# Attention, two expert layers: the order in which a pair's sums and reciprocals are emitted

## The chip, the core and the metric

The kernel runs on one core of one Trainium2 chip. The metric is the device time of one execution in microseconds (us), the median of the runs shown. A core has a matrix engine (PE, with its weight loads listed as PEld), a vector engine (DVE), an activation engine (ACT), a general engine (POOL) and a queue that issues transfers (SP). Each of them works through its own list of instructions in order and waits where an input or a buffer is not there yet.

## What is computed

Attention over 4 batches and 12 heads, with sequences of 448 and heads of 64, comes first. Its output, read as 1792 tokens of 768, goes through a dense two-layer network and then through one that sends each token to one of 8 experts. The change touches only the attention:

```python
def rmsnorm(x, g):
    rms = np.sqrt(np.mean(x * x, axis=-1, keepdims=True) + 1e-06)
    return x / rms * g
q_n, k_n = (rmsnorm(q, g_q), rmsnorm(k, g_k))
scores = scale * np.matmul(q_n, k_n.transpose(0, 1, 3, 2))
scores = scores - np.max(scores, axis=-1, keepdims=True)
attn = np.exp(scores)
attn = attn / (np.sum(attn, axis=-1, keepdims=True) + 1e-09)
return np.matmul(attn, v).astype(np.float32)
```

## The kernel before, in words

The attention works on 24 pairs of heads. The 448 keys of a pair lie in four chunks of 112. One pass of the loop in `pieces` (lines 363 to 383) walks through the names in `ORDER` (line 385), and each name emits a piece of work for one of several pairs: the current one, the one before it, the next one, or one further ahead.

- `Uk` and `Uq` (`turn_k`, `turn_q`, lines 228 to 244) turn the normalised keys and queries of the pair two passes ahead on PE into a PSUM buffer named `tr` (line 225). ACT copies the high part (`kh` L242, `qh` L233), and DVE takes the low part (`kl` L243, `ql` by the helper on L63).
- `P0` to `P3` (`probs`, line 262) make the scores of one chunk of the current pair: eight PE matmuls into the one `sc` buffer (L273; `SCB` is 1) and the exponential on ACT (L275). The first chunk's result goes into `pr`, the other three into `p`.
- `V0` to `V3` (`values`, line 278) multiply a chunk's probabilities with the values on PE (L284) into `av`. From the second chunk on POOL adds `p` to `pr` (L288). So a pair has three additions, the last one behind `P3`.
- `S` (`sums`, line 290) belongs to the pair before. PE sums `pr` over the keys (L296, 16 small matmuls into a `tr` buffer), ACT copies the result (L300), PE brings it back into columns (L303), and DVE takes the reciprocals `r` (L306).
- `C` (`close`, line 309) belongs to the pair before too. PE spreads `r` (L314, 16 small matmuls into a `tr` buffer), ACT copies it (`rt`, L318), DVE multiplies `av` with it (L320), ACT and DVE split the result into a high and a low part (`xTh` L322, `xTl` on L63).
- `T0` to `T3` (`top`, L250 and L252) find the maxima of the scores of the next pair: two PE matmuls into the one `tp` buffer and a DVE reduction. `R` (`row`, L257 and L259) turns the maxima by way of a `tr` buffer.
- `A` (line 366) prepares later pairs: loads of q, k and v on SP (L173, L174), squares on ACT (`sq`, L192) and their sums on DVE (`ms`, L193) for two pairs at a time, a chain of small DVE operations for the reciprocal root (L195 to L201) and the product on POOL (`qn`, L216). `sq` and `qn` share one tag with three buffers.

There are two `tr` buffers, used by `Uk`, `S`, `C`, `Uq` and `R` in turn, two `av` and two `pr` buffers. The text of the program gives the emission order; a scheduler places the instructions on the engines, and emission order ranks them. In the last six passes the attention overlaps with the decoding of weights for the dense network (`decode`, line 399), whose first transfers are emitted behind the last load of the attention (line 646).

Of the kernel before, what the change touches and what calls it, by code (L numbers as in the profile page):

```python
# [20 lines left out]
def attention_moe_moe2(  # L21
# [17 lines left out]
    B, H, S, DH = q.shape  # L39
# [111 lines left out]
    class Attention:  # L151
# [173 lines left out]
        def pieces(self):  # L325
# [37 lines left out]
            for i in range(n + 1):  # L363
                for op in ORDER:
                    cur, prev, nxt = (sts[m] if 0 <= m < len(sts) else None for m in (i, i - 1, i + 1))
# [16 lines left out]
                        self.row(nxt)  # L382
                    yield

    ORDER = "Uk P0 S P1 C V0 T0 P2 V1 T1 P3 Uq V2 A T2 T3 R V3".split()
    BANK, HALVES = 512, (slice(0, DH), slice(DH, P))
    SCB, AVB, TRB = 1, 2, 2
    QK, VV, PB, RT, WD, RAW, D0, DS, NU, L0, LA, U0, US, LW, XL, SD = 3, 2, 3, 1, 1, 3, 18, 2, 2, -2, 2, 5, 4, 3, 1, 0
# [254 lines left out]
    for i, _ in enumerate(att.pieces()):  # L643
        step = i // len(ORDER)
        if step >= D0 and i % (DS * len(ORDER)) == 0 and len(wts.raw) < RAW:
            wts.decode(att.last)
# [298 lines left out]
```

## Time and profile before

| what | value |
|---|---|
| median of 3 runs | 1267.56 us (1266.53 to 1269.69) |
| the profiled execution, its time | 1269.48 us |
| its span from first to last instruction | 1267.8 us |
| granted TensorE clock, mean | 0.974 of full speed |
| stretch in which the attention runs steadily | about 94 to 302 us of the span |
| dense network, steady | about 500 to 880 us |
| expert network | about 920 to 1268 us |

The profile lists for each engine when an instruction was busy, how long the engine stood idle before it, and which instruction's end released it. An idle gap costs time only where the work behind it lies on the path that sets the end. A wait for several things is put down to the one that came last.

### The profile page before, as it was taken

To read this page: it belongs to the slowest core of one execution; us is meant where nothing else is said; L and a number is where in the kernel's file an instruction comes from. 1 tells how busy PE (TensorE), PEld (TensorE's weight loads), DVE (VectorE), ACT (ScalarE), POOL (GpSimd) and SP (SyncE) were. 2 spreads that over 40 slices of the span, in tenths; PEclk is the share of its full clock that TensorE was granted. 3 is DMA by queue.
4 is the path that set the end of the run, shared out by engine and by line. 5 is a ranking of instruction groups with operands and counts; after the bars stand their busy time and mean duration, and the time that the engine had idled before them with its cause. 6 is when DMAs were issued, how large, how long until landed. Compare 5 with 4: busy or idle time off the path is not lost.

```text
span 1267.8 us, 19050 instructions
## 1 busy us (share of the span) xinstructions
PE 1173.1 (93%) x6988; PEld 935.8 (74%) x6988; DVE 783.3 (62%) x1291; ACT 500.9 (40%) x791; POOL 544.1 (43%) x366
## 2 busy tenths in 40 slices
PE   4899998989888998999999999999799999999997
PEld 2445554545466887898989898988678888898986
DVE  7576777766765788485858584335656159414456
ACT  3355655555433532222222222122335158314444
POOL 2656666766553554343434443120224136312334
PEclk9889999999888999999999999999889999999999
DMA  4112111210222222021202120062276039512556
GB/s 103 51 50 62 45 52 44 59 37 16 65 63 63 75 78 72 13 75 38 70 31 75 38 63 1 1 218 59 74 283 223 34 120 359 210 46 84 185 214 219
DMA packets 68081, 116.28 MB, mean 92 GB/s; under 512 B 6780, under 2 KB 45948, under 8 KB 67968
## 3 DMA queue, kind: packets, MB, share of 16 engines
q1 hardware_dynamic: 64848, 103.87, 25.6%
q0 software_dynamic: 3120, 11.02, 2.5%
q8 instruction: 57, 0.93, 0.3%
q14 instruction: 56, 0.46, 0.1%
HBM read 106.61 MB, written 12.58 MB: 94 GB/s over the span
## 4 chain that ended last, share of the span: by engine, by line
PE 61%; DVE 17%; POOL 8%; issue 5%; ACT 4%; DMA 3%; SPq 1%; ACTq 0%; DVEq 0%; POOLq 0%
PE mp L485 5%; PE mo L466 5%; PE mp L486 5%; PE mo L467 5%; PE mp L487 5%; PE mo L468 5%; PE ph L823 4%; PE ph L822 3%; PE ph L821 3%; PE sc L273 3%; PE av L284 3%; PE py L839 3%; PE py L837 3%; PE py L838 3%; POOL pr L288 2%
## 5 line engine op out<-in xcount | busy, mean ns | idle before, releaser
L288 POOL TENSOR_TENSOR pr<-pr,p 112x896 f32<-112x896 f32 x72 | 160.2, 2225 | 89.9 <-ACT p L275 81.5
L493 DVE TENSOR_TENSOR ysum<-mp,ysum 128x448 f32<-128x448 f32 x168 | 103.6, 620 | 114.9 <-PE mp L487 114.0
L485 PE MATMUL mp<-gh,w1h 128*128 128x448 f32 x384 | 144.9, 379 | 15.5 <-DVE ysum L493 12.8
L466 PE MATMUL mo<-xTh,w0h 128*128 128x448 f32 x384 | 143.3, 373 | 4.8 <-DVE g L473 4.6
L486 PE MATMUL mp<-gl,w1h 128*128 128x448 f32 x384 | 142.7, 372 | 0.0
L467 PE MATMUL mo<-xTl,w0h 128*128 128x448 f32 x384 | 142.3, 370 | 0.0
L468 PE MATMUL mo<-xTh,w0l 128*128 128x448 f32 x384 | 142.1, 370 | 0.0
L487 PE MATMUL mp<-gh,w1l 128*128 128x448 f32 x384 | 141.4, 371 | 0.1
L63 POOL TENSOR_TENSOR gl<-g,gh 128x448 fp32r<-128x448 f32 x64 | 78.0, 1218 | 134.8 <-ACT gh L474 107.5
L252 DVE TENSOR_REDUCE md<-tp 112x2 f32<-112x896 f32 x96 | 104.3, 1087 | 18.4 <-PE tp L250 18.4
L425 POOL TENSOR_TENSOR raw<-raw,top 128x384 f32<-128x384 f32 x64 | 64.8, 1012 | 114.1 <-DVE raw L423 111.6
L837 PE MATMUL py<-w2h,hT 128*128 128x384 f32 x288 | 99.7, 346 | 0.0
L839 PE MATMUL py<-w2l,hT 128*128 128x384 f32 x288 | 96.8, 336 | 0.0
L838 PE MATMUL py<-w2h,hL 128*128 128x384 f32 x288 | 96.5, 335 | 0.0
L485 PEld LDWEIGHTS mp<-gh,w1h 128*128 128x128 f32 x384 | 73.0, 190 | 29.0 <-DVE ysum L493 14.8
L63 DVE TENSOR_TENSOR hL<-pt,hT 128x512 fp32r<-128x512 f32 x36 | 24.8, 689 | 106.2 <-ACTq L847 59.3
L823 PE MATMUL ph<-w1l,xgh 128*128 128x512 f32 x216 | 86.3, 400 | 4.2 <-DVE w1l L63 4.2
L275 ACT ACTIVATE p<-sc 112x896 f32<-112x896 f32 x72 | 65.8, 914 | 53.7 <-PE sc L273 53.4
L821 PE MATMUL ph<-w1h,xgh 128*128 128x512 f32 x216 | 86.6, 401 | 0.3 <-ACT xgh L799 0.3
L419 ACT ACTIVATE mag<-wd 128x384 f32<-128x384 f32 x64 | 35.5, 555 | 128.6 <-DVE raw L426 109.7
L822 PE MATMUL ph<-w1h,xgl 128*128 128x512 f32 x216 | 85.5, 396 | 0.0
L466 PEld LDWEIGHTS mo<-xTh,w0h 128*128 128x128 f32 x384 | 72.9, 190 | 13.5 <-DVE g L473 6.3
(195 smaller groups left out, 2567.4 us busy)
## 6 DMA issues: line engine op xcount, KB each, us to landing
r<-in_moe_w_dram SPq DMA_DIRECT2D x27, 1024.0 KB, 5.3
r<-in_moe_w_dram SPq DMA_DIRECT2D x36, 768.0 KB, 7.4
wd<-in_moe_w_in_dram SPq DMA_DIRECT2D x32, 384.0 KB, 3.3
wd<-in_moe_w_out_dram SPq DMA_DIRECT2D x32, 384.0 KB, 3.0
qk<-in_q_dram SPq DMA_DIRECT2D x24, 224.0 KB, 2.9
qk<-in_k_dram SPq DMA_DIRECT2D x24, 224.0 KB, 3.2
vv<-in_v_dram SPq DMA_DIRECT2D x24, 224.0 KB, 3.0
x2d<-xn SPq DMA_DIRECT2D x24, 224.0 KB, 2.9
```

The costliest lines, as they stand in the source:

```text
L288: nc.gpsimd.tensor_tensor(st["pr"][:CP], st["pr"][:CP], p, ALU.add)
L466: nc.tensor.matmul(ph, wh_[:, c], xh, start=(c == 0), stop=False)
L467: nc.tensor.matmul(ph, wh_[:, c], xl, start=False, stop=False)
L468: nc.tensor.matmul(ph, wl_[:, c], xh, start=False, stop=(c == KD - 1))
L485: nc.tensor.matmul(py, hi[:, sl], gh, start=(j == 0), stop=False)
L486: nc.tensor.matmul(py, hi[:, sl], gl, start=False, stop=False)
L487: nc.tensor.matmul(py, lo[:, sl], gh, start=False, stop=(j == GF - 1))
L821: nc.tensor.matmul(ph[n], xh[:, c], w1h[:, c, s_], start=(c == 0), stop=False)
L823: nc.tensor.matmul(ph[n], xh[:, c], w1l[:, c, s_], start=False, stop=(c == K1 - 1))
L837: nc.tensor.matmul(py[n], hT[:, c], w2h[:, c, s_], start=(c == 0), stop=False)
L838: nc.tensor.matmul(py[n], hL[:, c], w2h[:, c, s_], start=False, stop=False)
L839: nc.tensor.matmul(py[n], hT[:, c], w2l[:, c, s_], start=False, stop=(c == K2 - 1))
```

## The change

One line differs. `S` moves from behind `P0` to behind `P2`. `C` moves from behind `P1` to behind `Uq`, which itself follows `P3`. No operation is added or removed.

```diff
-    ORDER = "Uk P0 S P1 C V0 T0 P2 V1 T1 P3 Uq V2 A T2 T3 R V3".split()
+    ORDER = "Uk P0 P1 V0 T0 P2 S V1 T1 P3 Uq C V2 A T2 T3 R V3".split()
```

## Rows read from the trace of the kernel before

**Rows 1.** The page: busy time of the engines over the span.
```profile
PE 1173.1 (93%) x6988; PEld 935.8 (74%) x6988; DVE 783.3 (62%) x1291; ACT 500.9 (40%) x791; POOL 544.1 (43%) x366
```

**Rows 2.** Busy time by stretch; the first line names the columns.
```profile
core 0: us, PE busy (x) PEld busy (x) DVE busy (x) ACT busy (x) POOL busy (x), PEclk, DMA share, GB/s
94.00:302.00 208.00, 189.16 (x1632) 106.28 (x1632) 151.07 (x250) 117.07 (x169) 135.14 (x77) 1.00 0.17 48
...
500.00:880.00 380.00, 372.75 (x1929) 333.90 (x1928) 223.47 (x418) 94.11 (x167) 130.51 (x103) 1.00 0.19 57
```

**Rows 3.** All waits of PE from 94 to 302 us: sum, times, longest.
```profile
PE tr L296 <- POOL pr L288: 14.6, 16, 1.5
PE tr L314 <- DVE r L306: 4.2, 7, 0.6
```

**Rows 4.** Timeline of PE, one pass from 200.44 us (start, duration, operation).
```profile
201.15 0.36 PE L273 MATMUL sc<-mx,mask 64*112 64x448 f32 x2
201.35 0.37 PE L250 MATMUL tp<-kh,qh 64*112 64x448 f32 x2
203.24 0.59 PE L296 MATMUL tr<-pr,ones_mat 113*32 113x112 f32 x16 [1.53 <-POOL pr L288]
203.76 0.46 PE L273 MATMUL sc<-qh,kh 64*112 64x448 f32 x2
...
205.67 0.55 PE L303 MATMUL av<-ident,sp 128*112 128x4 f32 x4
...
208.16 0.94 PE L314 MATMUL tr<-ident,r 112*64 112x112 f32 x16
209.03 0.60 PE L225 MATMUL tr<-ident,qn 112*128 112x112 f32 x4
...
211.66 0.60 PE L257 MATMUL tr<-ident,md 112*128 112x112 f32 x4
212.20 0.46 PE L250 MATMUL tp<-kh,qh 64*112 64x448 f32 x2
212.59 0.60 PE L225 MATMUL tr<-ident,qn 112*128 112x112 f32 x4
```

**Rows 5.** Timeline of PE, from a pass of the other kind.
```profile
161.71 0.59 PE L296 MATMUL tr<-pr,ones_mat 113*32 113x112 f32 x16 [0.46 <-POOL pr L288]
...
167.60 0.60 PE L314 MATMUL tr<-ident,r 112*64 112x112 f32 x8 [0.61 <-DVE r L306]
```

**Rows 6.** Timeline of POOL.
```profile
194.66 2.04 POOL L216 TENSOR_TENSOR qn<-qk,y 112x512 f32<-112x512 f32 x2 [1.03 <-DVE y L201]
196.67 2.10 POOL L288 TENSOR_TENSOR pr<-pr,p 112x896 f32<-112x896 f32 x1
198.72 2.44 POOL L216 TENSOR_TENSOR qn<-qk,y 112x512 f32<-112x512 f32 x2
201.12 2.07 POOL L288 TENSOR_TENSOR pr<-pr,p 112x896 f32<-112x896 f32 x1
...
212.58 2.92 POOL L288 TENSOR_TENSOR pr<-pr,p 112x896 f32<-112x896 f32 x1 [1.88 <-ACT p L275]
```

**Rows 7.** Timeline of ACT.
```profile
203.96 0.35 ACT L300 COPY sp<-tr 128x224 f32<-128x224 f32 x1 [1.49 <-PE tr L296]
204.93 0.92 ACT L275 ACTIVATE p<-sc 112x896 f32<-112x896 f32 x1 [0.63 <-PE sc L273]
...
209.67 0.55 ACT L233 ACTIVATE qh<-tr 128x448 fp32r<-128x448 f32 x1
210.11 1.05 ACT L192 ACTIVATE sq<-qk 112x1024 f32<-112x1024 f32 x1
```

**Rows 8.** Timeline of DVE.
```profile
206.26 0.21 DVE L306 RECIPROCAL r<-av 112x8 f32<-112x8 f32 x1 [3.41 <-PE av L303]
...
209.72 0.62 DVE L320 TENSOR_TENSOR rt<-av,rt 128x448 f32<-128x448 f32 x1 [1.98 <-ACT rt L318]
...
212.92 0.62 DVE L63 TENSOR_TENSOR xTl<-rt,xTh 128x448 fp32r<-128x448 f32 x1
...
217.80 0.20 DVE L200 TENSOR_TENSOR a<-a,hm 112x32 f32<-112x32 f32 x1
...
218.48 2.12 DVE L200 TENSOR_TENSOR a<-a,hm 112x32 f32<-112x32 f32 x1
...
221.31 0.19 DVE L201 SCALAR_TENSOR_TENSOR y<-a,y 112x32 f32<-112x32 f32 x1
```

**Rows 9.** The chain of waits where the decoding of weights begins.
```profile
318.76 0.93 PE av L284 x4
319.70 0.31 SPq L174
320.01 0.05 issue
320.06 3.76 DMA wd<-in_moe_w_in_dram
```

## The prediction

> **What bounds the kernel now.** I read the page first: PE is the fullest engine over the span [rows 1]. Then I cut the span into stretches. From 94 to 302 us, where the attention runs at the full granted clock, PE is busy 189.16 of 208.00 us and no other engine passes 151.07 [rows 2]. The reader is to see that PE stands idle for 18.84 us there. The waits of PE over the same stretch name all of it: 14.6 us before the sums (L296), for POOL's addition L288, and 4.2 us before the spreading (L314), for the reciprocals L306 [rows 3]. Together 18.8 us. These are the two pieces that the change moves, so 18.8 us is the most that the steady attention can give while PE's own work stays as it is.
>
> The timelines say where the waits come from. Passes come in two kinds, by turns, because the squares and roots of two pairs are done at once. In the first kind PE waits 1.53 us before the sums [rows 4]: POOL had put two pairs of normalising products `qn` between the additions, 2.04 and 2.44 us, and the last addition ran only from 201.12 for 2.07 us [rows 6]. In the second kind the wait is 0.46 us, and the spreading then waits 0.61 us for `r` [rows 5]. There the last addition had no product ahead of it; it started at 212.58 when its exponential was there, and took 2.92 us [rows 6].
>
> **How the order on the engines comes about.** It isn't the emission order. In [rows 4] a score maximum (201.35), emitted far behind the sums, runs ahead of them, and they run ahead of the second score chunk (203.76). I read this as: what has its inputs goes first, and emission only ranks what is ready together. The second chunk can't be ready early, since it needs the one `sc` buffer, which the first exponential frees. The `tr` buffers look different. The keys turned at 212.59 had their `qn` at 198.72 plus 2.44 = 201.16 [rows 6], and yet PE turned them 11 us later, right behind `R` at 211.66 [rows 4]. So I take it that `tr` buffers are handed out in order of emission: `Uk`, `S`, `C`, `Uq`, `R` before, `Uk`, `S`, `Uq`, `C`, `R` after.
>
> **The change part by part.**
>
> *The sums move behind the third chunk.* Nothing is added: the 16 matmuls (0.59 us), the copy (0.35), the return (0.55) and the reciprocal (0.21) stay [rows 4, 7, 8]. No DMA and no POOL instruction moves with them. By the reading above they are still ready while the first exponential runs and still rank ahead of the later maxima, so their place on PE stays. Bounds: no gain at all, or, where emission order does hold, the whole 14.6 us, because the last addition ends at 203.19 and PE would come to the sums only behind chunk two, `V0` and chunk three. I take neither end, but what the next step does to POOL.
>
> *The spreading moves behind `Uq`.* This is the edit that acts. `Uq` is free of the spreading, which waits for `r`, and needs only a `tr` buffer that `kl` gave back long before. It can move from 209.03 to the neighbourhood of the sums, up to 5 us earlier. PE pays nothing for that, its work is only reordered. ACT's `qh` follows (0.55 us), and with it `sq` (1.05 us), which in [rows 7] starts directly behind `qh`: both follow the end of the same turning, which also gives back a `qn` buffer. ACT has 1.49 and 0.63 us idle there [rows 7], 2.12 against 1.60 of new work, so I cost it at nothing; if it doesn't fit, one exponential per two passes comes up to 1.05 us late, which the `V0`, return and maxima behind chunk two cover for the most part. On DVE the sums of squares and the start of the root chain move into idle gaps of 3.41 and 1.98 us [rows 8] and out of the row of work without a gap that ends with `y` at 221.50. `y` comes earlier, and so do the `qn` products on POOL, which then no longer stand ahead of the last addition in the first kind of pass.
>
> The price of that wait is bounded by 0 and 1.53 us. I take 0.46, the row that is nearest: the same addition without a product ahead of it [rows 5]. The stretch has eight passes of each kind. Eight waits of 0.46 make 3.7 us in the second kind, so 14.6 - 3.7 = 10.9 us fall to the first. These 10.9 become 3.7: a gain of 7.2 us.
>
> The wait of the spreading: `r` came 0.61 us late. `Uq` (0.60 us on PE) now runs ahead of it and PE arrives that much later, while `r` is not later. The 4.2 us go [rows 3]; bounds 0 and 4.2.
>
> What `Uq` used to hide is late next: the spreading's own followers (`rt`, L320, `xTh`, `xTl`) come some 0.6 us later. Nobody waits soon: the `av` buffer is wanted a pass later, and the keys' turning, which now takes over the spreading's `tr` buffer, comes 2.9 us after L320's start at 209.72. I cost this at 0, with the second rival as the bound above.
>
> *After the attention.* The decoding begins with a transfer queued behind a load of values, which waits for a buffer freed by `V3` at 318.76 [rows 9]. It moves along with the attention, and from 500 us on PE is busy 372.75 of 380 [rows 2]; I pass the gain on whole.
>
> **Sum.** 7.2 + 4.2 = 11.4 us off. The profiled execution took 1269.48 us (span 1267.8), 1.92 above the median; 1269.48 - 11.4 = 1258.1, and on the scale of the median 1267.56 - 11.4 = 1256.2.
>
> **The rivals.**
>
> *The order holds as written* (chance 0.15). Sums run behind chunk three, spreading behind chunk four. All of 18.8 us goes: 1248.8. For it: the program says so. Against: the maxima that overtake the sums [rows 4].
>
> *It doesn't do what it says* (0.18). Sums stay, the turning and the spreading only change places, the `qn` products stay where they are. Then POOL's block from 194.66 to 203.19 still gates the sums, and the loop back to it by DVE keeps its length. Gain 0 to 0.46 per first-kind pass, 0 to 3.7 us: 1264 to 1267.6. For it: the first-kind wait closes such a loop, and a 0.61 us gap off it would be worth nothing.
>
> *Slower, the products go ahead of the last addition in both kinds* (0.21). Where `y` is ready before the fourth exponential, POOL takes a product first, as it does at 198.72 [rows 6], and the first pair's product lands in the second kind too. Decisive is whether `y` comes before about 212.5, the start of the last addition there. Then all 16 sums wait 1.53 us: 24.5 in place of 14.6, so 9.9 more, and 1277.5.
>
> *Slower by the shared operands* (0.09). A DVE product of two SBUF operands took 0.20 us at 217.80 and 2.12 at 218.48, while POOL's addition ran, and POOL's last addition took 2.92 where another took 2.07 [rows 6, 8], while `xTl` ran at 212.92. With the spreading later, `xTl` falls on the last addition in the first kind as well: 0.85 us more, eight times, 6.8 us: 1274.4. The Trainium skill (SBUF — State Buffer, Who interferes with whom) has the rule: a DVE instruction with two SBUF inputs and a GpSimd instruction that reads SBUF block each other for a whole instruction. The 2.12 us agrees with it.
>
> **How the numbers follow.** The forecast has 0.37, with a range of its own from 1253.5 (three quarters of the 18.8 us gone) to 1263.4 (only the spreading's wait gone). Cases of both signs hold the chance, so the whole range runs from 1244 (the second case less some 5 us, for the waits before 94 us that the steady stretch doesn't count) to 1276, short of the third rival's end. A measurement of this kernel tells about 0.3%, 3.8 us, from no change. Faster: 0.37 + 0.15 = 0.52. Same: 0.18. Slower: 0.21 + 0.09 = 0.30.
>
> **What would show it.** Right: L225 with `qh` behind it runs ahead of L314 and near L296; `sq` with it; `y` and the `qn` products earlier against the additions; PE's wait before L296 half as long in sum, before L314 gone; L296 still between the first and second chunk. Wrong: L296 behind the third chunk (first rival), the same POOL order (second), or waits before L296 of 1.5 us in every pass (third), or a new PE wait on `sc` or a `tr` buffer.

## The result, and the profile after

| what | before | after |
|---|---|---|
| median of five runs each | 1268.41 us (1266.53 to 1269.69) | 1280.37 us (1275.87 to 1285.54) |
| the profiled execution, its time | 1269.48 us | 1279.04 us |
| its span | 1267.8 us | 1277.3 us |
| granted clock, mean | 0.974 | 0.973 |

The kernel became about 1% slower: the ratio is 1.0099, with a 95% interval from 1.0079 to 1.0118. The forecast was 1256.2 us, a gain, and its range ended at 1276. Both were wrong.

The busy time by stretch of the kernel after answers to [rows 2]; the columns are the same.

```profile
94.00:302.00 208.00, 189.06 (x1530) 103.14 (x1526) 154.16 (x232) 109.51 (x161) 120.30 (x72) 0.97 0.15 44
500.00:880.00 380.00, 370.72 (x1895) 332.24 (x1894) 229.60 (x420) 95.25 (x168) 135.50 (x107) 1.00 0.19 58
```

PE is as full as before in the attention, 189.06 us against 189.16, but with 1530 recorded instructions in place of 1632: the same 208 us hold less work. The mean granted clock fell from 1.00 to 0.97 there. All waits of PE in that stretch, as in [rows 3]:

```profile
PE tp L250 <- DVE md L252: 11.3, 8, 1.6
PE tr L257 <- DVE md L252: 7.6, 7, 1.1
```

The two waits that the change was to remove are gone, all 18.8 us of them. Two others stand in their place, both for the maxima `md` that DVE reduces, and their sum is 18.9 us. The timeline of PE shows where they lie (start, duration, operation, and in brackets the wait ahead of it).

```profile
193.16 0.32 PE L257 MATMUL tr<-ident,md 112*128 112x112 f32 x1 [1.08 <-DVE md L252]
...
195.41 0.37 PE L273 MATMUL sc<-mx,mask 64*112 64x448 f32 x2
197.36 0.46 PE L250 MATMUL tp<-kh,qh 64*112 64x448 f32 x2 [1.58 <-DVE md L252]
197.75 0.59 PE L296 MATMUL tr<-pr,ones_mat 113*32 113x112 f32 x16
198.27 0.60 PE L225 MATMUL tr<-ident,qn 112*128 112x112 f32 x4
198.80 0.46 PE L273 MATMUL sc<-qh,kh 64*112 64x448 f32 x2
...
203.20 0.94 PE L314 MATMUL tr<-ident,r 112*64 112x112 f32 x16
204.06 0.41 PE L257 MATMUL tr<-ident,md 112*128 112x112 f32 x2
...
204.79 0.31 PE L257 MATMUL tr<-ident,md 112*128 112x112 f32 x1
...
210.06 0.59 PE L296 MATMUL tr<-pr,ones_mat 113*32 113x112 f32 x16
210.58 0.60 PE L225 MATMUL tr<-ident,qn 112*128 112x112 f32 x4
```

The queries (L225 at 198.27 and 210.58) are turned right behind the sums, about 5 us ahead of the spreading (L314 at 203.20), as forecast. The sums still lie between the first score chunk (its last matmuls at 195.41) and the second (198.80). They start at 197.75, at 210.06, and again at 225.53: two passes, called a double pass from here on, take 27.78 us. Before, the same starts were 203.24 and, two passes on, 230.16: 26.92 us. The second kind of pass costs 12.31 us in both kernels; the first grew from 14.61 to 15.47.

The chain of waits over the longer pass, from 210 us on, names the path (start, duration, what).

```profile
210.65 0.55 PE tr L225 x4
...
211.66 1.06 ACT sq L192
...
212.74 1.22 DVE ms L193
...
214.08 1.02 DVE md L252
215.09 1.23 DVE ms L193
...
216.34 1.81 DVE ms L195
...
219.35 0.54 DVE rt L320
219.88 1.00 DVE md L252
...
221.65 1.99 DVE a L199
...
224.08 1.01 DVE md L252
```

The reader is to see a loop. The turning of the queries releases the squares, the squares release the root chain on DVE, three maxima stand between the steps of that chain in DVE's list, and the last maximum, at 224.08, releases L250 and with it the next sums and the next turning of queries. Two of the small operations on 112x32 values take 1.81 and 1.99 us; the same forms take 0.17 to 0.20 elsewhere. The timeline of POOL one double pass earlier says beside what.

```profile
188.23 2.10 POOL L288 TENSOR_TENSOR pr<-pr,p 112x896 f32<-112x896 f32 x1 [0.30 <-ACT p L275]
193.66 2.14 POOL L288 TENSOR_TENSOR pr<-pr,p 112x896 f32<-112x896 f32 x1 [3.34 <-ACT p L275]
196.38 2.04 POOL L216 TENSOR_TENSOR qn<-qk,y 112x512 f32<-112x512 f32 x2 [0.58 <-DVE y L201]
198.95 2.04 POOL L216 TENSOR_TENSOR qn<-qk,y 112x512 f32<-112x512 f32 x2 [0.53 <-PE tr L225]
```

In the first kind of pass no product stands ahead of the last addition (193.66) any more, as forecast. The timeline of DVE beside it:

```profile
188.57 1.80 DVE L195 TENSOR_SCALAR ms<-ms 112x32 f32<-112x32 f32 x1
...
193.88 1.98 DVE L199 TENSOR_TENSOR a<-y 112x32 f32<-112x32 f32 x1
...
196.22 1.08 DVE L252 TENSOR_REDUCE md<-tp 112x2 f32<-112x896 f32 x1
```

Each held-up operation starts just after an addition of POOL has started, and ends just after it: 188.57 + 1.80 = 190.37 against 188.23 + 2.10 = 190.33, and 193.88 + 1.98 = 195.86 against 193.66 + 2.14 = 195.80. Before, one operation per two passes was held up so, for 2.12 us [rows 8]; now two are, and a maximum that PE waits for stands behind each. The Trainium skill (SBUF — State Buffer, Who interferes with whom) says that the two-port form of a one-input operation (`tensor_scalar` can have one) also locks GpSimd and DVE against each other. The 1.80 us of the one-input L195 agree; that L195 ran in that form is not shown.

**Where the time went.** From the sums of pass 4 on, seven double passes take 200.67 us (94.30 to 294.97) against 188.47 before (95.54 to 284.01): 12.2 us more. Seven times 27.78 - 26.92 = 0.86 us make 6.0 of them. The other 6.2 lie in three passes that take 15.39, 13.87 and 13.86 us in place of 12.31. There the granted clock fell. The busy time by 4 us, around the first fall and around the same place of a double pass without one:

```profile
134.00:138.00 4.00, 2.41 (x30) 1.14 (x26) 3.93 (x6) 1.19 (x2) 3.42 (x3) 1.00 0.19 61
138.00:142.00 4.00, 4.00 (x26) 1.73 (x18) 1.38 (x2) 1.81 (x3) 2.27 (x3) 0.62 0.39 125
142.00:146.00 4.00, 4.00 (x18) 2.49 (x20) 1.30 (x2) 0.92 (x1) 2.09 (x1) 0.53 0.33 104
...
194.00:198.00 4.00, 2.42 (x26) 1.05 (x26) 3.93 (x6) 1.40 (x3) 3.42 (x3) 1.00 0.18 57
198.00:202.00 4.00, 4.00 (x44) 2.50 (x34) 2.10 (x4) 1.81 (x3) 3.47 (x4) 1.00 0.42 116
```

A granted 0.53 means that the engine ran almost all of that stretch at the lower of its two levels, 1.2 GHz. All three falls follow the place where both waits for `md` lie. The same place at 194 us, with the same 2.42 us of PE, was followed by none. So in this execution the falls come behind these two waits; why in three passes and not in the others, the rows don't tell. Nor are falls peculiar to these waits. In the first run of the experiments below, which has the old waits and none for `md`, one pass of the kind that takes 12.31 us took 15.44, with a granted clock of 0.80, 0.50 and 0.84 in the three stretches of 4 us from 146 us on. The 6.2 us are what the falls cost in this one execution.

Of the 0.86 us per double pass, the waits are only 0.09 (2.59 us before, 2.68 after). The rest is PE's own time: the time of a double pass less the waits in it was 24.33 us and is 25.10. The largest piece is the turning of the maxima (L257), counted from the start of each group to the next start on PE, less a wait: 1.07 us in two groups before (one of them is in [rows 4], x4) and 1.61 us in six groups after. Chopped up between other operations, the same eight transposes cost 0.54 us more. So against the kernel before, the new waits only take back what the old ones gave; the loss in the steady stretch is PE's own time and the clock.

From pass 21 to the end part of the loss is made good: the first L466 of the dense network comes 11.1 us later (363.6 against 352.5), the end 9.5 us later (1277.3 against 1267.8). Why was not traced.

### The profile page after: what moved, and what is told of

It is laid out like the page before. It is cut to its first block, busy times and chain, and to the rows that moved or that the text cites. A ratio compares the mean times of both kernels' runs of the same rounds, so it can differ in the third digit from the quotient of the medians.

```text
span 1277.3 us, 19009 instructions
## 1 busy us (share of the span) xinstructions
PE 1183.4 (93%) x6988; PEld 937.4 (73%) x6988; DVE 789.1 (62%) x1291; ACT 497.2 (39%) x791; POOL 533.0 (42%) x366
## 4 chain that ended last, share of the span: by engine, by line
PE 69%; DVE 16%; issue 4%; ACT 4%; POOL 3%; DMA 2%; SPq 1%; ACTq 0%; DVEq 0%; POOLq 0%
PE mp L485 6%; PE mo L466 6%; PE mo L467 5%; PE mp L486 5%; PE mo L468 5%; PE mp L487 5%; PE av L284 4%; PE sc L273 4%; PE ph L823 4%; PE ph L822 3%; PE ph L821 3%; PE py L839 3%; PE py L837 3%; PE py L838 3%; DVE md L252 2%
## 5 line engine op out<-in xcount | busy, mean ns | idle before, releaser
L288 POOL TENSOR_TENSOR pr<-pr,p 112x896 f32<-112x896 f32 x72 | 153.0, 2126 | 117.9 <-ACT p L275 78.5
L466 PE MATMUL mo<-xTh,w0h 128*128 128x448 f32 x384 | 142.8, 372 | 4.2 <-DVE g L473 3.9
L466 PEld LDWEIGHTS mo<-xTh,w0h 128*128 128x128 f32 x384 | 72.9, 190 | 12.7 <-DVE g L473 5.7
L63 POOL TENSOR_TENSOR w1l<-r,w1h 128x1024 fp32r<-128x1024 f32 x17 | 42.9, 2530 | 93.0 <-ACT w1h L785 76.0
```

The source lines that it names most:

```text
L63: engine.tensor_tensor(dst, src, hi.bitcast(F32), ALU.subtract)
L288: nc.gpsimd.tensor_tensor(st["pr"][:CP], st["pr"][:CP], p, ALU.add)
L466: nc.tensor.matmul(ph, wh_[:, c], xh, start=(c == 0), stop=False)
```

## The experiments

Ratios are against the kernel before on the same chip. The statements that follow were on record before each run.

**The place of the spreading: one word of the order.** The change with `Uq` and `C` exchanged:

```diff
-    ORDER = "Uk P0 P1 V0 T0 P2 S V1 T1 P3 Uq C V2 A T2 T3 R V3".split()
+    ORDER = "Uk P0 P1 V0 T0 P2 S V1 T1 P3 C Uq V2 A T2 T3 R V3".split()
```

> Sums behind P2 and spreading behind P3 as in the change, but the spreading still ahead of Uq. Theory 1 (the turn of the tr buffers decides, and the loss comes from Uq, and with it the squares, being free of the spreading): the order on PE, the waits of PE before L296 and L314 and the two-pass period of 26.9 us come back; 1264 to 1271 us. Theory 2 (the later emission of the sums or of the spreading costs by itself, through its followers rt, L320, xTh, xTl): as the change, 1276 to 1285 us.

Measured: 1264.69 us against 1267.68, ratio 0.9978 (0.996 to 0.9997), as theory 1 had it. The waits of PE from 94 to 302 us are those of before to within 0.3 us, two passes take 26.92 us again where the clock does not fall, and L257 is back in two groups:

```profile
PE tr L296 <- POOL pr L288: 14.3, 15, 1.5
PE tr L314 <- DVE r L306: 4.2, 7, 0.6
```

The reverse, only the spreading moved and the sums left behind `P0`:

```diff
-    ORDER = "Uk P0 P1 V0 T0 P2 S V1 T1 P3 Uq C V2 A T2 T3 R V3".split()
+    ORDER = "Uk P0 S P1 V0 T0 P2 V1 T1 P3 Uq C V2 A T2 T3 R V3".split()
```

> Only the spreading moves, behind Uq; the sums stay behind P0. Theory 1: as the change, with no wait of PE before L296 and L314, waits of 10 to 20 us before L250 and L257 from 94 to 302 us; 1276 to 1285 us. Theory 3 (the sums' later rank is the cause): as before, 1264 to 1271 us.

Measured: 1281.01 us, ratio 1.0117 (1.0089 to 1.0144), again as theory 1 had it: two passes in 27.79 us, PE's own part 25.11, and the waits of the change:

```profile
PE tp L250 <- DVE md L252: 11.4, 8, 1.6
PE tr L257 <- DVE md L252: 7.5, 7, 1.1
```

So the sums' place in the text does nothing, and the whole effect belongs to the turn of `Uq` and `C` at the `tr` buffers. This holds for the chopped turnings too. As I read it, with two buffers handed out in turn `R` takes the one of the piece two places ahead of it. That was `C`, whose copy `rt` came late; now it is `Uq`, which is done early. So `R` has its buffer before its maxima are there, and turns each as it comes.

**The order as written** (the first rival). Sums and spreading are held, by a dependence of issue alone, behind the last score product of the chunk that stands ahead of them in the text:

```diff
-                    nc.tensor.matmul(
+                    self.scored = nc.tensor.matmul(
...
-                        self.sums(prev)
+                        with tc.issue_after(self.scored.ins) if cur else ExitStack():
+                            self.sums(prev)
...
-                        self.close(prev)
+                        with tc.issue_after(self.scored.ins) if cur else ExitStack():
+                            self.close(prev)
```

> The change with its order enforced on PE: the sums queued behind the third chunk's last matmul and the spreading behind the fourth's. If the waits before L296 and L314 were all that stood in the way (first rival of the prediction): 1245 to 1258 us. If the sums, the return, the spreading and both turnings, squeezed behind chunk three, make the turned maxima late for the next pass (a new wait of the first chunk's last matmuls on mx): 1268 to 1295 us.

Measured: 1332.03 us, ratio 1.0498 (1.0479 to 1.0517), beyond both ranges. PE waits for the exponentials now, passes take 13.8 and about 20 us, and the clock is 0.85:

```profile
PE av L284 <- ACT p L275: 11.7, 6, 2.0
PE tp L250 <- DVE md L252: 10.1, 12, 1.8
PE sc L273 <- ACT pr L275: 5.5, 12, 0.6
```

The order that the text writes is no gain: were it followed, the kernel would be slower by 5%.

**When the squares run.** `sq` gets a buffer of its own and no longer shares with `qn`, in the change and in the kernel before:

```diff
-                sq = self.early.tile([CP, n, DH], F32, name="sq", tag="qn", bufs=3)
+                sq = self.early.tile([CP, n, DH], F32, name="sq", bufs=1)
```

> The change's order, but the squares have a buffer of their own and don't share three with qn. Theory 1: the squares no longer start behind Uq, both at once in every second pass; the closed loop Uq, squares, sums of squares, root chain, maxima, sums, Uq is cut, the waits before L250 and L257 fall from 18.9 us to under 8, the two-pass period falls from 27.8 us to 24.5 to 26; 1245 to 1266 us. Theory 2: the period stays at 27.8, 1276 to 1285 us. If the two blocked small DVE operations per two passes are the cause wherever the squares stand: period 26.5 to 27.8, 1265 to 1283 us.

> The order of before, with a buffer of its own for the squares. Theory 1: the squares come one in each pass and earlier; the wait before L296 (14.6 us from 94 to 302) changes, since the products on POOL move; 1252 to 1270 us. If the shared buffers do not gate the squares: no change, 1264 to 1271 us with the same order.

Measured: 1326.34 us, ratio 1.0469 (1.0435 to 1.0503), and 1319.54 us, ratio 1.0413 (1.0383 to 1.0443). Neither run gave what was expected of it. The timeline of ACT in the first shows why:

```profile
204.03 1.06 ACT L192 ACTIVATE sq<-qk 112x1024 f32<-112x1024 f32 x1 [4.20 <-DMA qk<-in_k_dram]
204.99 0.90 ACT L275 ACTIVATE p<-sc 112x896 f32<-112x896 f32 x1
...
219.33 1.06 ACT L192 ACTIVATE sq<-qk 112x1024 f32<-112x1024 f32 x1 [3.37 <-DMA qk<-in_k_dram]
```

Without the shared buffer the squares are placed ahead of the exponential in ACT's list, and wait there for their load: ACT stands idle for 4.20 us with the exponential behind them. PE then waits for exponentials (L273, 14.1 us from 94 to 302 in the first run and 14.8 in the second). The shared tag is what kept the squares out of the way.

The other way round: the change with the squares queued behind the spreading's copy `rt`, as late as before:

```diff
-                    nc.scalar.activation(sq[:, h], flat[:, h], AF.Square)
+                    with tc.issue_after(self.turned_rt.ins) if self.turned_rt else ExitStack():
+                        nc.scalar.activation(sq[:, h], flat[:, h], AF.Square)
...
-            nc.scalar.activation(rt, tr, AF.Copy)
+            self.turned_rt = nc.scalar.activation(rt, tr, AF.Copy)
```

> The change's order; on ACT the squares are queued behind the copy rt of the spreading (L318), some 5 us later than in the change and about where they stood before. Everything on PE keeps the change's order. Theory 1 (the squares' early start puts the root chain where its small DVE operations are held up behind POOL's additions, with the maxima behind them): waits of PE before L250 and L257 from 94 to 302 us fall from 18.9 to under 9 us, period 24.5 to 26.9 us, 1250 to 1270 us. Theory 4 (the early turning of the queries itself, with the maxima's turning ahead of the fourth chunk on PE, makes these waits): period 27.5 or more, 1274 to 1285 us.

Measured: 1287.57 us, ratio 1.0147 (1.0129 to 1.0165). The waits for `md` are gone, all of them, with the queries still turned early, so they hang on the early squares and not on the early turning by itself. The time was a miss for both theories: theory 1 had 1250 to 1270 us, and theory 4, whose period came, had the waits for `md` stay. The wait for POOL's last addition is back, in every pass and up to 2.0 us long (the sums are on L297 and the additions on L289 here):

```profile
PE tr L297 <- POOL pr L289: 22.4, 14, 2.0
```

In one kind of pass the products are ahead of the additions again: four run from 186.59 us for 4.54, two additions behind them end at 195.35, and the sums start at 195.40. In the other kind no product is ahead; the last addition starts with its exponential and takes 3.09 us. So with early squares PE waits for maxima behind the root chain, and with late squares it waits for additions, in every second pass behind the products.

**Without the refinement of the root.** The root chain keeps its first guess, and its three refinement steps (nine small operations on DVE per two pairs) are left out, in the change and in the kernel before:

```diff
-            for _ in range(3):
+            for _ in range(0):
```

> The change without the three refinement steps of the reciprocal root (nine small DVE operations per two passes are left out, the roots stay at their first guess). Theory 1: the DVE chain from the squares to the next maxima sets the period; with one of its two hold-ups and nine operations gone (3.6 us of 27.8) PE's waits for maxima fall under 6 us, period 24.4 to 25.8 us, 1245 to 1262 us. If the DVE chain is not on the path: 1276 to 1285 us.

> The kernel before without the same refinement steps. Theory 1: there the chain sets when the products on POOL start; PE's wait before L314 goes, that before L296 falls or moves; 1250 to 1264 us, so that the change's loss against its own counterpart is gone or turned round. If the chain is not on the path: 1264 to 1271 us.

Measured: 1246.31 us, ratio 0.9826 (0.9808 to 0.9844), and 1238.87, ratio 0.9754 (0.9737 to 0.9771). In the change the waits fall from 18.9 to 4.0 us:

```profile
PE tr L296 <- POOL pr L288: 2.7, 8, 1.1
PE tr L257 <- DVE md L252: 1.1, 6, 0.2
PE tp L250 <- DVE md L252: 0.2, 1, 0.2
```

The chain was on the path in both kernels. L195 is still held up here, for 1.80 us in every double pass (at 190.38, say), yet PE waits for a maximum by at most 0.2 us: this hold-up makes PE wait only together with the refinement steps behind it. The kernel before gained more than expected, and the change's loss against it, which theory 1 had gone or turned round, remained: the change stays 7.4 us slower. Two passes take 25.34 us against 24.86; PE's own part is 24.92 against 24.11, with L257 in six groups against two. This is the part of the loss that has nothing to do with DVE: 0.81 us per double pass, of which shorter waits (0.42 against 0.75 us) give back 0.33. Over eight double passes it accounts for 3.9 of the 7.4 us; the rest lies ahead of and behind the steady passes and was not traced.

**Without the additions on POOL** (`pr` keeps its first chunk, so the sums are over a quarter of the keys):

```diff
-            if c:
-                nc.gpsimd.tensor_tensor(st["pr"][:CP], st["pr"][:CP], p, ALU.add)
```

> The change with POOL's additions L288 left out, so that the sums are over the first chunk alone. Theory 1, with the hold-ups behind the additions as its size: no DVE operation of the root chain lasts 1.8 us or more, PE's waits before L250 and L257 from 94 to 302 us fall from 18.9 to under 4 us, period 24.3 to 25.2 us, and the time is within 4 us of its counterpart without additions in the old order. If the length of the chain without hold-ups is enough to make the maxima late: waits before L250 and L257 over 8 us, and over 6 us slower than the counterpart.

> The kernel before with the same additions left out. PE's wait before L296 goes with them; period 24.3 to 25.2 us, 1236 to 1254 us.

Measured: the change 1323.95 us, ratio 1.0429 (1.0411 to 1.0446); the kernel before 1235.81, ratio 0.9737 (0.9717 to 0.9756). In the change every small operation of the root chain now takes 0.17 to 0.20 us, so it is the additions that hold the chain up. The waits for `md` fall to 2.7 us. The time of this run was a miss: a new wait of 21.3 us for the exponential came up (L273), since on ACT `xTh` stood ahead of it and waited 3.78 us for `rt`, which stood behind all of the root chain but its last operation on DVE. With the engines' lists changed that much, neither the time nor the waits for `md` tell what the hold-ups cost by themselves, apart from the refinement steps. An estimate from the rows of the change: each hold-up adds more than the wait behind it, 1.80 - 0.17 = 1.63 us against 1.08, and 1.98 - 0.19 = 1.79 us against 1.58. In the kernel before, where the sums no longer wait for POOL, PE is busy 205.31 of the 208 us.

**The refinement steps on POOL.** There they can't collide with POOL's additions. Each step takes four operations in place of three:

```diff
-                nc.vector.tensor_tensor(a, yf, yf, ALU.mult)
-                nc.vector.tensor_tensor(a, a, hm, ALU.mult)
-                nc.vector.scalar_tensor_tensor(yf, a, 1.5, yf, ALU.add, ALU.mult)
+                nc.gpsimd.tensor_tensor(a, yf, yf, ALU.mult)
+                nc.gpsimd.tensor_tensor(a, a, hm, ALU.mult)
+                nc.gpsimd.tensor_scalar(a, a, 1.5, None, ALU.add)
+                nc.gpsimd.tensor_tensor(yf, a, yf, ALU.mult)
```

> The change with the refinement steps of the root on POOL, four operations each, in place of three on DVE: they stand in the same list as the additions and so can't be held up behind one on another engine, and the maxima on DVE no longer stand behind them. Theory 1: waits before L250 and L257 fall under 8 us; POOL has 12 more short operations per two passes, so a wait before L296 may come back; 1248 to 1272 us. If the maxima are late for another reason: 1274 us or more with waits before L250 and L257 over 12 us.

> The kernel before with the same refinement steps on POOL. Theory 1: the products on POOL start behind the steps instead of behind DVE's row of work; the wait before L296 stays or grows, that before L314 goes; 1252 to 1275 us. In the old order the steps on DVE cost by way of POOL, so the gain, if there is one, is smaller than with the new order.

Measured: in the change's order 1270.69 us, ratio 1.0012 (0.9994 to 1.003); in the order of before 1289.73 us, ratio 1.0159 (1.0138 to 1.0181), where 1252 to 1275 had been expected. The sign of the change turns: with the steps off DVE its order is 19 us faster than the old one. Two passes take 25.83 us. But the first passes, up to 106 us, were slow: the intervals between sums are 19.81, 19.35 and 14.38 us against 14.95, 15.87 and 12.32 in the change. So three more runs kept the steps of the first pairs on DVE, the first two of them those of five pairs (`hp` under 5), the third those of seven (`hp` under 6, as printed):

```diff
+                if sts[0]["b"] == 0 and sts[0]["hp"] < 6:
+                    nc.vector.tensor_tensor(a, yf, yf, ALU.mult)
+                    nc.vector.tensor_tensor(a, a, hm, ALU.mult)
+                    nc.vector.scalar_tensor_tensor(yf, a, 1.5, yf, ALU.add, ALU.mult)
+                else:
...
```

> The change with the refinement steps on POOL (four operations each) only for the pairs from the sixth on; the first five keep them on DVE as before. With all steps on POOL the change took 1270.69 us, and its passes before 94 us were slow (19.8, 19.4, 14.4 us against 15.0, 15.9, 12.3), although its steady passes were 13.06 and 12.76. Theory 1 (the change loses by the refinement steps on DVE and by nothing else; what was left in the earlier run was the start): the start comes back to that of the change, the steady passes stay at 25.8 us per two, about 1.95 us per two under the change for eight double passes, and the falls of the clock are gone: 1280.4 - 1.95 x 8 - 6 = some 1259, under the kernel before. Theory 2 (the slow start is made good later, as part of the change's loss is): no difference to the earlier run, 1268 to 1272.

> The same edit in the order of before. With all steps on POOL that order took 1289.7 us, with a wait before the sums of 15.7 us in 9 passes and passes of 11 to 17 us. Theory 1 (in this order the steps on POOL stand between the additions that the sums wait for, in the steady passes): still slower than the kernel before by over 10 us, 1278 to 1290. Theory 2 (its loss too came from the start): within 5 us of the kernel before.

> The change with the refinement steps on POOL only for the pairs from the eighth on, so one group of two pairs later than in the run with the sixth. Theory 1 (the steady passes carry the gain, each double pass about 1.95 us): one double pass less, 1 to 3 us over that run. Theory 2 (the sixth pair still lies in the start, where POOL's steps are late): 2 to 6 us under that run.

Measured, the change's order with five pairs on DVE: 1272.73 us, ratio 1.0026 (1.0004 to 1.0049), a miss for theory 1 and near theory 2: the steady passes were as expected, but an early pass still took 19.72 us, and one more 14.05. The order of before with five pairs on DVE: 1295.51 us, ratio 1.0212 (1.0176 to 1.0249), the loss of theory 1 and past its range. The change's order with **seven pairs on DVE: 1257.94 us, ratio 0.9913 (0.9879 to 0.9947)**. Its first intervals are 12.87, 13.39 and 12.76 us, so the slow start is gone. It beats both kernels, by 22 us the changed one; part of that is the start, which is faster than the change's (14.95, 15.87 and 12.32 us). That the one group of pairs is worth 14.8 us was more than either theory had said. Its busy time from 94 to 302 us:

```profile
94.00:302.00 208.00, 199.83 (x1670) 110.35 (x1668) 153.26 (x183) 118.65 (x174) 160.74 (x175) 1.00 0.15 45
```

And all waits of PE there (the sums are L302, the additions L294, the maxima L258 in this kernel):

```profile
PE tr L302 <- POOL pr L294: 6.2, 15, 2.1
PE tr L263 <- DVE md L258: 1.7, 7, 0.2
PE tp L256 <- DVE md L258: 0.3, 1, 0.3
```

PE's waits are 8.2 us in place of 18.9, the clock is 1.00, and two passes take 25.81 us, of which PE's own part is 24.98: the turnings are still in six groups. L195 is still held up (1.80 us at 199.52), but of the root chain only two operations, of 0.18 and 0.17 us, stand between it and the next maximum (202.15), for which PE waits 0.25 us. The same split in the order of before closed the question:

> The order of before with the refinement steps on POOL from the eighth pair on, the same split that took the change's order to 1257.9 us. Theory 1 (the split only frees the start; in this order the steps on POOL stand ahead of the additions that the sums wait for, in every double pass): slower than the kernel before, 1283 to 1296, so that the change's order is worth 25 to 38 us once the steps are off DVE. Theory 2 (the late split is what gains, in either order): 1256 to 1266.

Measured: 1289.41 us, ratio 1.0188 (1.0157 to 1.0218), 31.5 us slower than the change's order with the same split (on two chips, on which the kernel before took 1266.99 and 1268.15 us). The timeline of POOL says why:

```profile
235.35 2.12 POOL L294 TENSOR_TENSOR pr<-pr,p 112x896 f32<-112x896 f32 x1
237.41 4.44 POOL L222 TENSOR_TENSOR qn<-qk,y 112x512 f32<-112x512 f32 x4
241.82 2.06 POOL L294 TENSOR_TENSOR pr<-pr,p 112x896 f32<-112x896 f32 x1
```

The squares come late in that order, so the steps and all four products stand ahead of the last addition, and the sums behind it (L302 at 243.93) wait 3.46 us.

## Why the prediction was wrong

- *"It isn't the emission order", and `tr` buffers are handed out in order of emission.* Right. The sums stayed between the first and the second chunk, the order as written was no gain, and exchanging two words brought the old kernel's passes back, to within 0.02 us where the clock did not fall.
- *The waits for the sums and for the spreading.* Right in direction, too small in size: 11.4 us were to go, and all 18.8 went. The `qn` products come earlier against the additions, as forecast.
- *"On DVE the sums of squares and the start of the root chain move into idle gaps", with no cost set on it.* **This is the step that failed.** The gaps were real [rows 8], but the prediction looked at how much DVE was idle and not at what stood behind the moved chain in DVE's list: the maxima that PE needs for L250 and L257. It also had the price of a hold-up in a row, 2.12 us [rows 8], and did not ask which additions of POOL the earlier chain would meet. It met two per double pass in place of one. The longer chain, steps and hold-ups together, made 18.9 us of new waits where 7.4 had been forecast to remain: 11.5 of the 24.2 us between the forecast and the measured time. Squares put late again removed them, and steps left out or moved off DVE took them down to 1.3 and 2.0 us.
- *"PE pays nothing for that, its work is only reordered."* The second step that failed, smaller: `R` got its `tr` buffer earlier and turned the maxima one by one, 0.77 us of PE's own time more per double pass in all, 5.4 us over seven double passes. The prediction followed `Uq` and `C` through the buffers but not `R`, the next in turn.
- *The clock.* Not in the sum at all. Falls to 1.2 GHz in three passes cost 6.2 us in the profiled execution, half of the loss in the steady stretch. That the change makes falls more frequent is not shown: in the same stretch the same waits went with one fall when only the spreading moved (a pass of 13.87 us), and the old waits with one and with none.
- *The rivals.* The slower one with the products ahead of the last addition (0.21) gave 1277.5, close to the 1280.4 measured, but by luck, since its mechanism did not occur: from 94 to 302 us PE waited for no addition. The one by shared operands (0.09) named the right mechanism at the wrong place: it had `xTl` lengthen an addition in the first kind of pass; in the traces additions hold up the root chain. The list of what would make it wrong named a new PE wait on `sc` or a `tr` buffer; the new waits were for `tp`, and for the maxima themselves.

## What to carry to other kernels

When a change makes a chain on another engine start earlier, read that engine's list behind the chain: idle time is no cover if something that the bound engine needs comes to stand behind it. Where buffers are handed out in turn, follow every user of the tag through the new order, the ones that the change doesn't name too. And an order and the placement of work on engines can't be judged apart: this order lost 12 us against the old one with the refinement steps on DVE and won 31.5 with them, from the eighth pair on, on POOL.

## What the runs showed of the hardware

A one-input operation on DVE, 112x32 in place, took 1.80 us behind an addition on POOL and 0.17 us without one. Eight transposes on PE cost 1.07 us in two groups and 1.61 us in six. And the granted clock fell in only three of the double passes with the two waits: of two stretches of 4 us with PE busy 2.41 and 2.42 us, one was followed by a fall and one was not. It fell once, too, behind a single wait of 1.53 us for an addition.
